# Two chunks of P moved to a load's wait; at the start, one cast given to ACT and the state's transposes split over two tiles

## Chip, cores, metric

One core of one Trainium2 chip. The metric is the device time of the whole kernel in microseconds (us); smaller is better. Where a run is traced, the profile's span is about 1.7 us shorter than the time of the same run.

## The reference, cut to what matters

```python
# x: [8, 8, 512, 64], state: [8, 8, 32, 64], w_in: [512, 2048], w_out: [2048, 512]
a     = softmax(scale * x @ state.T)        # per batch and head
xread = a @ state                           # 512 rows a batch
sread = softmax(scale * state @ x.T) @ x    # 32 rows a batch
y     = concat([xread, sread]) -> [8 * 544, 512]
out   = gelu(y @ w_in) @ w_out
```

The kernel never forms `xread`. It computes P = state @ w_in for each batch (2 x 128 rows by 2048 columns, in four chunks of 512), and then h = a @ P. So P chunks (batch b, quarter f) are small matmuls that must lie somewhere ahead of the h matmuls that read them. This is what the change moves.

## The kernel before

The program gives the order on each engine by itself; nothing is rescheduled. `M(i)` is one h tile (two full matmuls, then Gelu on ACT), `U(i)` and `mm2_m` are second-layer matmuls into `op`. PSUM has four banks for everything tagged `f`, taken in rotation, and four tagged `op`, which hold the open sums of batch 0.

```python
def scores(b, half):                       # tag f, freed by Exp on ACT
    pt = ps_f.tile([128, SJ, 2, 2, NS], FP32, name="pt", tag="f")
    ...                                    # 8 matmuls
    nc.scalar.activation(out=A.e[...], in_=pt..., func=AF.Exp, scale=scale)

def p_mm(b, f, pool, tag):                 # a chunk: 2 tiles, 8 matmuls of 64*32
    ps = [pool.tile([128, 512], FP32, name="p_ps", tag=tag) for t in range(2)]
    for c in range(HC):
        for t in range(2):
            nc.tensor.matmul(ps[t][32 * c:32 * c + 32, :], ...)
    return ps

def p_copy(b, f, ps):                      # each tile freed by its own engine
    dst = Ps[b][:, :, f * 512:(f + 1) * 512]
    nc.scalar.copy(out=dst[:, 0, :], in_=ps[0])
    nc.vector.tensor_copy(out=dst[:, 1, :], in_=ps[1])
...
    # start: batch 0
    keep_warm(32); cast0(0); xtr0(0)
    st0 = state0()        # 4 transposes + 1, one tile; ACT copies to sb0
    cast0(1); state0_p(st0); keep_warm(5)
    cast0(2); xtr0(1); xtr0(2); xtr0(3)
    scores0(0); ...
...
    # around the third w_out chunk (m = 8..11)
    xtr(1, (0, 1)); xtr(1, (2, 3)); rearr_ones(1)
    M(10, 11)
    mm2_m(0, 8)                            # first use of that chunk
    scores(1, 0); scores(1, 1)
    mm2_m(0, 9)
    burst([(0, 3), (1, 0)])
    norm(1, 0); norm(1, 1)                 # softmax on DVE
    mm2_m(0, 10); mm2_m(0, 11); M(12, 13); M(14, 15)
    ...
    sread(1); sread_out(1)                 # tile sr, freed by DVE's srm
    burst([(1, 1), (1, 2)])
    atr(1); U(12); srt(1); state_prep(2, B); U(13); M(16, 17); ...
```

The softmax here doesn't subtract the row's maximum and nothing guards it: scores larger than these inputs give would overflow.

Of the kernel before, what the change touches and what calls it, by code (L numbers as in the profile page):

```python
# [10 lines left out]
BF16 = mybir.dt.bfloat16  # L11
# [6 lines left out]
def kernel(  # L18
# [8 lines left out]
    nc = tc.nc  # L27

    B, H, S, D = x.shape
    _, _, NS, _ = state.shape  # L30
# [3 lines left out]
    HC = H // 2  # L34
# [10 lines left out]
    ps_f = ctx.enter_context(tc.tile_pool(name="ps_f", bufs=4, space=PSUM))  # L45
# [9 lines left out]
    sbd = persist.tile([128, B, HC, 2 * NS], BF16, name="sbd")  # L55
# [8 lines left out]
    sb0 = persist.tile([128, 2, 2, 2, NS], BF16, name="sb0")  # L64
# [80 lines left out]
    def keep_warm(n, m=128):  # L145
        for _ in range(n):
            nc.tensor.matmul(
                warm_ps[0:m, 0:128], lhsT=warm[:, 0:m], rhs=warm, start=True, stop=True
            )
# [20 lines left out]

    def state0():
        nc.scalar.copy(out=st_bf[:, 0, :, :], in_=st_f)
        ps = ps_f.tile([128, 3, HC, NS], BF16, name="st0_ps", tag="f")
        for t in range(2):
            for u in range(2):
                nc.tensor.transpose(
                    ps[64 * u:64 * u + 64, t, :, :].rearrange("p c n -> p (c n)"),
                    st_bf[:, 0, t, :],
                    ident,
                )  # L180
        nc.tensor.transpose(
            ps[:, 2, :, :].rearrange("p c n -> p (c n)"),
            st_bf[:, 0, :, :].rearrange("q t d -> q (t d)"),
            ident,
        )
        for u in range(2):
            h = slice(64 * u, 64 * u + 64)
            nc.scalar.copy(out=sb0[h, :, :, u, :], in_=ps[h, 0:2, u:HC:2, :])
        return ps

    def state0_p(ps):
        for t in range(2):
            h = slice(64 * t, 64 * t + 64)
            nc.scalar.copy(out=sbd[h, 0, :, 32 * t:32 * t + 32], in_=ps[h, 2, :, :])


    class Att:
# [28 lines left out]
    def rearr_ones(b):  # L226
        A = atts[b]
        eng = nc.vector if b < 2 else nc.gpsimd
        src = xbs[b].rearrange("p (t c) (j d) -> p t c j d", t=2, d=D)
        for t in range(2):  # L230
            eng.tensor_copy(  # L231
                out=A.xo[:, :, :, 2 + 64 * t:66 + 64 * t].rearrange("p j c d -> p c j d"),
                in_=src[:, t],
            )


    def cast0(q):
        nc.vector.tensor_copy(
            out=x0b[:, q, :, :, :].rearrange("p j u d -> p u j d"),
            in_=x0f[:, q, :, :].rearrange("p u (j d) -> p u j d", d=D),  # L240
        )
# [11 lines left out]
    def xtr0(q):  # L253
        ps = ps_f.tile([128, SJ, 128], BF16, name="xT_ps", tag="f")
        for j in range(SJ):
            if q < 3:
                nc.tensor.transpose(
                    ps[:, j, :], x0b[:, q, j, :, :].rearrange("p u d -> p (u d)"), ident
                )
                continue  # L260
            for u in range(2):
                nc.tensor.transpose(
                    ps[64 * u:64 * u + 64, j, :], x0c[:, u, D * j:D * j + D], ident
                )
        nc.vector.tensor_copy(out=xT0[:, q, :, :], in_=ps)
# [85 lines left out]
    def scores(b, half):  # L351
        A = atts[b]
        pt = ps_f.tile([128, SJ, 2, 2, NS], FP32, name="pt", tag="f")
        for ci in range(2):
            c = 2 * half + ci
            for j in range(SJ):
                nc.tensor.matmul(  # L357
                    pt[:, j, :, ci, :],
                    lhsT=A.xT[:, j, c, :],
                    rhs=sbd[:, b, c, :],  # L360
                    start=True,
                    stop=True,
                )
        nc.scalar.activation(  # L364
            out=A.e[:, :, 64 * half:64 * half + 64],
            in_=pt.rearrange("p j t c n -> p (j t) (c n)"),
            func=AF.Exp,
            scale=scale,
        )
# [17 lines left out]
    def atr(b, ts=(0, 1)):  # L387
        A = atts[b]
        if 0 in ts:
            A.AT = att.tile([128, SJ, 2, 128], BF16, name="AT", tag="AT")  # L390
        for t in ts:
            ps = ps_f.tile([128, SJ, 128], BF16, name="aT_ps", tag="f")
            for j in range(SJ):
                nc.tensor.transpose(ps[:, j, :], A.a[:, 2 * j + t, :], ident)
            nc.vector.tensor_copy(out=A.AT[:, :, t, :], in_=ps)
# [9 lines left out]
    def sread(b):  # L405
        A = atts[b]
        pool, tag = (ps_o, "op") if b == B - 1 else (ps_f, "f")
        A.sr = pool.tile([128, 2, 65], FP32, name="sr", tag=tag)
        for t in range(2):
            for j in range(SJ):  # L410
                for c in range(HC):
                    nc.tensor.matmul(  # L412
                        A.sr[32 * c:32 * c + 32, t, :],
                        lhsT=A.e[:, 2 * j + t if b else SJ * t + j, 32 * c:32 * c + 32],
                        rhs=A.xo[:, j, c, 1 + 65 * t:66 + 65 * t],
                        start=(j == 0),
                        stop=(j == SJ - 1),
                    )

    def sread_out(b):  # L420
        A = atts[b]
        A.srm = att.tile([128, 2, D], BF16, name="srm", tag="srm")
        flat = A.sr.rearrange("q t d -> q (t d)")
        inv = att.tile([128, 2], FP32, name="inv", tag="inv")
        nc.vector.reciprocal(out=inv, in_=flat[:, 0:130:129])
        nc.vector.tensor_tensor(
            out=A.srm,
            in0=flat[:, 1:129].rearrange("q (t d) -> q t d", t=2),
            in1=inv[:, :].to_broadcast((128, 2, D)),
            op=ALU.mult,  # L430
        )
# [11 lines left out]
    def p_mm(b, f, pool, tag):  # L443
        if b not in Ps:
            Ps[b] = att.tile([128, 2, d_ff], BF16, name="P", tag="P")
# [3 lines that stand above are left out]
                nc.tensor.matmul(  # L449
                    ps[t][32 * c:32 * c + 32, :],  # L450
                    lhsT=sbd[64 * t:64 * t + 64, b, c, 32 * t:32 * t + 32],
                    rhs=w_in_bf[64 * t:64 * t + 64, c, f * 512:(f + 1) * 512],
                    start=True,
                    stop=True,
                )
        return ps

    def p_copy(b, f, ps):
# [3 lines that stand above are left out]
# [7 lines left out]
    def burst(chunks, reads=()):  # L469
        done = []  # L470
        first = len(chunks) < 4
        if first:
            for b in reads:
                sread(b)
        for i, (b, f) in enumerate(chunks):
            pool, tag = (ps_f, "f") if i < 2 else (ps_o, "op")
            done.append((b, f, p_mm(b, f, pool, tag)))
        for x in done[:2]:
            p_copy(*x)
        if not first:  # L480
            for b in reads:
                sread(b)
        for x in done[2:3]:
            p_copy(*x)
        for b in reads:
            sread_out(b)
        for x in done[3:]:
            p_copy(*x)
# [114 lines left out]
    def mm2_m(b, m):  # L603
        for j in range(SJ):
            if m == 0:
                ops[b, j] = ps_o.tile([128, d_model], FP32, name="op", tag="op")
            nc.tensor.matmul(  # L607
                ops[b, j],
                lhsT=gs[b][:, m, j * 128:(j + 1) * 128],
                rhs=w_out_bf[:, m, :],  # L610
                start=(m == 0),
                stop=(m == MC - 1),
            )


    def M(*ms):
        for m in ms:
            mm1(m // MC, m % MC)

    def U(*us):  # L620
        for u in us:
            mm2(u // 16, u % 16 // 4, u % 4)

    begin(0)
    keep_warm(32)
    cast0(0)
    xtr0(0)
    st0 = state0()
    cast0(1)
    state0_p(st0)  # L630
    keep_warm(5)
    cast0(2)
    xtr0(1)
    xtr0(2)
    xtr0(3)
    scores0(0)
# [44 lines left out]
    begin(1)  # L681
    xtr(1, (0, 1))
    xtr(1, (2, 3))
    rearr_ones(1)
    M(10, 11)
    mm2_m(0, 8)
    scores(1, 0)
    scores(1, 1)
    mm2_m(0, 9)
    burst([(0, 3), (1, 0)])  # L690
    norm(1, 0)
    norm(1, 1)
    mm2_m(0, 10)
# [7 lines left out]
    rearr_ones(2)  # L701
    sread(1)
    sread_out(1)
    burst([(1, 1), (1, 2)])
    atr(1)
    U(12)
    srt(1)
    state_prep(2, B)
    U(13)
# [8 lines left out]
    u = 17  # L718
# [77 lines left out]
```

## Time and profile before

Median 216.37 us (216.16 to 216.68, 4 runs). PE is busy for 98% of the span. Three spots matter, in us from the span's start:

| what | where | size |
|---|---|---|
| PE's weight loads wait for batch 1's x, ahead of its transposes | 23.49 | 0.33 as the profile counts it; the matmuls 0.07 |
| PE waits for the third w_out chunk | 25.54 to 26.45 | 0.91 |
| PE waits inside the burst (1,1),(1,2) for PSUM banks | ends 34.37 | 0.81 as the profile counts it |

The prediction shows the lines for these. In the timeline, a row is start, busy time, engine, line, operation, tiles, forms, count, and in brackets the idle time before it. A row's busy time has holes in it if matmuls of the group waited: this is how the bank wait looks in PE's timeline of the kernel before.

```profile
33.37 1.41 PE L449 MATMUL p_ps<-w_in_bf,sbd 64*32 64x512 bf16 x16
34.70 0.64 PE L394 MATMUL aT_ps<-ident,a 128*128 128x128 bf16 x8
```

Sixteen P matmuls take from 33.37 to 34.70 here, and about 0.6 where nothing holds them. Two banks hold them in turn: the ninth matmul starts alone at 33.94, 0.06 after Gelu of m=15 ends (33.88), and the last seven at 34.37, after DVE's srm (34.31).

```profile
23.07 0.22 PE L156 MATMUL st_ps<-ident,st_bf 128*128 128x128 bf16 x1
23.22 1.08 PE L279 MATMUL xT_ps<-ident,xb 128*64 128x128 bf16 x32
```

### The profile page before, as it was taken

How to read it: one execution, taken by the hardware profiler on the slowest of the kernel's cores; microseconds unless marked ns; L12 is line 12 of the kernel's file. 1: busy time of each engine (PE TensorE's matmuls, PEld its weight loads, DVE VectorE, ACT ScalarE, POOL GpSimd, SP SyncE). 2: the span in 40 equal slices, each digit the busy share in tenths (PEclk: the TensorE clock that was granted, in tenths of full speed). 3: DMA queues.
4: the chain of work that ended last, by engine and by line, in shares of the span. 5: the costliest groups of instructions: out<-in, count | busy, mean ns of one | idle time of the engine just before them, and what ended most of it. 6: DMA issues, size and time to landing. Idle time of an engine off the chain costs nothing.

```text
span 214.9 us, 4080 instructions
## 1 busy us (share of the span) xinstructions
PE 209.7 (98%) x1700; PEld 103.1 (48%) x1700; DVE 79.8 (37%) x173; ACT 121.9 (57%) x216; POOL 43.5 (20%) x58
## 2 busy tenths in 40 slices
PE   8999899999999999999999999999999999999994
PEld 7634444444545444444444454444444444765443
DVE  4721559723049302850078005910393025000151
ACT  2754685696676447944874477645954444864000
POOL 7935204901113013301312121300000000000000
PEclk9999999999999999999999999999999999999999
DMA  6999999992723492428540872261232004000044
GB/s 183 183 203 194 207 190 150 197 244 52 98 98 101 81 143 41 177 41 134 74 173 25 148 96 108 90 129 20 77 123 52 0 26 173 0 0 3 6 106 181
DMA packets 41187, 23.24 MB, mean 108 GB/s; under 512 B 23120, under 2 KB 37712, under 8 KB 41168
## 3 DMA queue, kind: packets, MB, share of 16 engines
q0 software_dynamic: 14208, 8.23, 28.0%
q1 hardware_dynamic: 26272, 14.36, 24.8%
q10 hardware_dynamic: 688, 0.39, 0.6%
q8 instruction: 13, 0.21, 0.4%
q14 instruction: 6, 0.05, 0.1%
HBM read 17.30 MB, written 8.91 MB: 122 GB/s over the span
## 4 chain that ended last, share of the span: by engine, by line
PE 84%; DMA 10%; DVE 2%; POOL 2%; issue 1%; ACT 0%; POOLq 0%
PE op L562 45%; PE hp L513 23%; DMA w_out_bf<-in_moe_w_out_dram 10%; PE p_ps L449 4%; PE hps L577 3%; PE ops L589 3%; PE opl L540 2%; PE pt L357 2%; PE sr L412 1%; POOL w_in_bf L101 1%; PE op L607 1%; DVE a L380 1%; DVE P L461 1%; DVE cs L377 1%; POOL x0c L85 0%
## 5 line engine op out<-in xcount | busy, mean ns | idle before, releaser
L562 PE MATMUL op<-w_out_bf,g 128*128 128x512 bf16 x448 | 106.3, 379 | 0.0
L520 ACT ACTIVATE g<-hp 128x512 bf16<-128x512 f32 x124 | 66.4, 599 | 54.8 <-PE hp L513 54.7
L562 PEld LDWEIGHTS <-g 128*128 128x128 bf16 x448 | 43.6, 98 | 51.9 <-issue 0.8
L513 PE MATMUL hp<-AT,P 128*128 128x512 bf16 x248 | 63.1, 379 | 0.0
L526 DVE COPY osb<-op 128x512 f32<-128x512 f32 x31 | 21.4, 692 | 83.3 <-PE op L562 83.2
L513 PEld LDWEIGHTS <-P 128*128 128x128 bf16 x248 | 23.1, 98 | 26.0 <-ACT P L460 0.4
L461 DVE CAST P<-p_ps 128x512 bf16<-128x512 f32 x31 | 20.0, 683 | 12.4 <-PE p_ps L449 12.3
L460 ACT CAST P<-p_ps 128x512 bf16<-128x512 f32 x31 | 16.4, 595 | 12.5 <-PE p_ps L449 12.5
L221 POOL COPY x<-xb 128x1024 bf16<-128x1024 bf16 x12 | 12.1, 1041 | 33.3 <-DMA xb<-in_x_dram 28.3
L231 POOL COPY xo<-xb 128x1024 bf16<-128x1024 bf16 x12 | 12.2, 1046 | 21.3 <-PE sr L412 21.3
L607 PE MATMUL op<-w_out_bf,g 128*128 128x512 bf16 x48 | 11.5, 380 | 1.0 <-DMA w_out_bf<-in_moe_w_out_dram 0.9
L449 PE MATMUL p_ps<-w_in_bf,sbd 64*32 64x512 bf16 x248 | 11.0, 381 | 0.1
L377 DVE TENSOR_REDUCE cs<-e 128x16 f32<-128x512 bf16 x14 | 9.5, 677 | 3.7 <-ACT e L364 3.7
L380 DVE TENSOR_TENSOR a<-e,ics 128x512 bf16<-128x512 bf16 x14 | 9.7, 692 | 0.5
L364 ACT ACT_TABLE_LOAD x7 | 9.0, 1283 | 1.4 <-issue 1.3
L526 DVE COPY osb<-ops 128x512 f32<-128x512 f32 x2 | 1.4, 692 | 22.5 <-PE ops L589 22.5
L520 ACT ACT_TABLE_LOAD x7 | 9.0, 1283 | 0.1
L551 ACT COPY osb<-opl 128x128 f32<-128x128 f32 x1 | 0.3, 266 | 15.2 <-PE opl L540 15.2
L364 ACT ACTIVATE e<-pt 128x512 bf16<-128x512 f32 x14 | 7.6, 594 | 0.3 <-PE pt L357 0.2
L577 PE MATMUL hps<-XSR,w_in_bf 128*128 128x256 bf16 x64 | 7.6, 273 | 0.0
L607 PEld LDWEIGHTS <-g 128*128 128x128 bf16 x48 | 4.3, 98 | 7.0 <-issue 2.1
L449 PEld LDWEIGHTS <-sbd 64*32 64x32 bf16 x248 | 3.5, 89 | 7.6 <-issue 5.6
(85 smaller groups left out, 122.9 us busy)
## 6 DMA issues: line engine op xcount, KB each, us to landing
out_dram<-osb SPq DMA_DIRECT2D x25, 256.0 KB, 2.3
xb<-in_x_dram POOLq DMA_DIRECT2D x7, 512.0 KB, 6.3
w_out_bf<-in_moe_w_out_dram POOLq DMA_DIRECT2D x4, 512.0 KB, 11.9
w_in_bf<-in_moe_w_in_dram POOLq DMA_DIRECT2D x6, 256.0 KB, 11.8
out_dram<-osb SPq DMA_DIRECT2D x12, 128.0 KB, 2.1
x0f<-in_x_dram SPq DMA_DIRECT2D x2, 256.0 KB, 3.3
w_in_bf<-in_moe_w_in_dram POOLq DMA_DIRECT2D x4, 128.0 KB, 4.5
out_dram<-osb SPq DMA_DIRECT2D x8, 64.0 KB, 1.7
```

The source lines that it names most:

```text
L221: nc.gpsimd.tensor_copy(out=A.x4[:, :, :, 64 * t:64 * t + 64].rearrange("p j c d -> p c j d"), in_=src[:, t],)
L231: eng.tensor_copy(out=A.xo[:, :, :, 2 + 64 * t:66 + 64 * t].rearrange("p j c d -> p c j d"), in_=src[:, t],)
L364: nc.scalar.activation(out=A.e[:, :, 64 * half:64 * half + 64], in_=pt.rearrange("p j t c n -> p (j t) (c n)"), func=AF.Exp, scale=scale,)
L449: nc.tensor.matmul(ps[t][32 * c:32 * c + 32, :], lhsT=sbd[64 * t:64 * t + 64, b, c, 32 * t:32 * t + 32], rhs=w_in_bf[64 * t:64 * t + 64, c ...
L460: nc.scalar.copy(out=dst[:, 0, :], in_=ps[0])
L461: nc.vector.tensor_copy(out=dst[:, 1, :], in_=ps[1])
L513: nc.tensor.matmul(hp, lhsT=Ps[b][:, t, m * 128:(m + 1) * 128], rhs=atts[b].AT[:, :, t, :], start=(t == 0), stop=(t == 1),)
L520: nc.scalar.activation(out=gs[b][:, m, :], in_=hp, func=AF.Gelu)
L526: nc.vector.tensor_copy(out=osb, in_=ps)
L562: nc.tensor.matmul(ps, lhsT=gs[b][:, m, j * 128:(j + 1) * 128], rhs=w_out_bf[:, m, :], start=(m == 0), stop=(m == MC - 1),)
L577: nc.tensor.matmul(hp, lhsT=w_in_bf[:, c, m * 128:(m + 1) * 128], rhs=XSR[:, c, :], start=(c == 0), stop=(c == HC - 1),)
L607: nc.tensor.matmul(ops[b, j], lhsT=gs[b][:, m, j * 128:(j + 1) * 128], rhs=w_out_bf[:, m, :], start=(m == 0), stop=(m == MC - 1),)
```

## The change

The intent: put independent work, chunks (1,0) and (1,1), where PE stands waiting for w_out; drop the later burst that ran into held banks, by giving its chunk (1,2) to the burst of (0,3); and shorten the start by giving one of batch 0's casts to ACT and by splitting the state's transposes over two tiles, so that scores need not wait for all five.

```diff
     # start
-        ps = ps_f.tile([128, 3, HC, NS], ...)      # 5 transposes, one tile
+        ps = ps_f.tile([128, 2, HC, NS], ...)      # 4 transposes; the fifth in state0_p
...
-        nc.vector.tensor_copy(                     # cast0
+        copy = nc.scalar.copy if q == 1 else nc.vector.tensor_copy
+        copy(
...
-    state0_p(st0)
-    keep_warm(5)
+    state0_copy(st0)
+    keep_warm(6)
     cast0(2)
     xtr0(1)
+    state0_p()
     xtr0(2)
...  # P chunks
-    rearr_ones(1)
     M(10, 11)
+    burst([(1, 0), (1, 1)])
     mm2_m(0, 8)
     scores(1, 0)
     scores(1, 1)
+    rearr_ones(1)
     mm2_m(0, 9)
-    burst([(0, 3), (1, 0)])
+    burst([(0, 3), (1, 2)])
...
     sread_out(1)
-    burst([(1, 1), (1, 2)])
+    U(12)
     atr(1)
-    U(12)
     srt(1)
```

More of the change, by code (lines that the diff above doesn't have):

```diff
@@ L172, in state0 @@
         nc.scalar.copy(out=st_bf[:, 0, :, :], in_=st_f)
-        ps = ps_f.tile([128, 3, HC, NS], BF16, name="st0_ps", tag="f")
+        ps = ps_f.tile([128, 2, HC, NS], BF16, name="st0_ps", tag="f")
         for t in range(2):
@@ L180, in state0, with state0_copy, state0_p @@
                 )
+        return ps
+    def state0_copy(ps):
+        for u in range(2):
+            h = slice(64 * u, 64 * u + 64)
+            nc.scalar.copy(out=sb0[h, :, :, u, :], in_=ps[h, :, u:HC:2, :])
+    def state0_p():
+        ps = ps_f.tile([128, HC, NS], BF16, name="st0p_ps", tag="f")
         nc.tensor.transpose(
-            ps[:, 2, :, :].rearrange("p c n -> p (c n)"),
+            ps.rearrange("p c n -> p (c n)"),
             st_bf[:, 0, :, :].rearrange("q t d -> q (t d)"),
@@ L185, in state0 @@
         )
-        for u in range(2):
-            h = slice(64 * u, 64 * u + 64)
-            nc.scalar.copy(out=sb0[h, :, :, u, :], in_=ps[h, 0:2, u:HC:2, :])
-        return ps
-    def state0_p(ps):
         for t in range(2):
             h = slice(64 * t, 64 * t + 64)
-            nc.scalar.copy(out=sbd[h, 0, :, 32 * t:32 * t + 32], in_=ps[h, 2, :, :])
+            nc.scalar.copy(out=sbd[h, 0, :, 32 * t:32 * t + 32], in_=ps[h, :, :])
     class Att:
```

## The prediction

> **What bounds the kernel now.** I read the page first, then the chain of work that ended last, then the timeline engine by engine up to 46 us, and last the landing times of the loads from the views of their tiles. The page's first part and three rows of the view of stretches say it in short:
>
> ```profile
> PE 209.7 (98%) x1700; PEld 103.1 (48%) x1700; DVE 79.8 (37%) x173; ACT 121.9 (57%) x216; POOL 43.5 (20%) x58
> ...
> 10.60:25.50 14.90, 14.86 (x109) 6.42 (x106) 4.54 (x12) 7.62 (x16) 5.67 (x8) 1.00 1.29 201
> 25.50:26.50 1.00, 0.09 (x2) 0.04 (x1) 0.63 (x2) 0.98 (x3) 0.00 (x0) 1.00 1.25 212
> 26.50:34.40 7.90, 7.76 (x104) 3.35 (x103) 4.83 (x11) 7.03 (x11) 0.00 (x0) 1.00 1.53 193
> ```
>
> The columns are the stretch, its length, then busy time of PE, weight loads, DVE, ACT and POOL, the clock, the DMA share and GB/s. PE is busy in every stretch except 25.5 to 26.5 us, and the DMA engines are full throughout (about 200 GB/s). From 37.3 us to the end the chain is PE alone, back to back, so a matmul that starts x earlier at 37 us makes the kernel x shorter. The question is only what the change is worth between 0 and 37 us. The pieces of the chain that decide it, and the waits behind them:
>
> ```profile
> 12.20 14.22 DMA w_out_bf<-in_moe_w_out_dram
> 26.41 0.04 issue
> 26.45 1.02 PE op L607 x4
> ```
>
> ```profile
> PEld L449 <- DVE srm L426: 0.8, 1, 0.8
> PE op L607 <- DMA w_out_bf<-in_moe_w_out_dram: 0.9, 1, 0.9
> ```
>
> ```profile
> 26.25 1.28 ACT L364 ACT_TABLE_LOAD   x1
> 27.75 1.08 ACT L364 ACTIVATE e<-pt 128x512 bf16<-128x512 f32 x2 [0.21 <-PE pt L357]
> 29.36 1.07 ACT L460 CAST P<-p_ps 128x512 bf16<-128x512 f32 x2 [0.53 <-PE p_ps L449]
> 30.45 1.28 ACT L520 ACT_TABLE_LOAD   x1
> ```
>
> PE waits in two places. At 25.54 it waits 0.91 us for the third w_out chunk, issued at 12.20 and landed at 26.41. In the later burst of P chunks (1,1) and (1,2), which starts at 33.37, it stands still until 34.37: the last of that burst's four PSUM tiles takes the buffer that sread's result holds until DVE has written srm, and DVE is late because of the softmax work before it. ACT, 7.03 us busy of 7.90, is the second thing to watch in that stretch.
>
> **What the Trainium skill says.** (1) "ScalarE: Activation LUTs", section "What ACT_TABLE_LOAD costs": about 1283 ns for a switch of set, and a drain of about 1380 ns on top. The trace agrees with the first (1.28 us) and not with the second: the load at 30.45 ends at 31.73 and Gelu starts at 31.82. Copies load no table here (the casts at 29.36 follow Exp directly). (2) "TensorE: Matmul & The Clock Gate", section "Part 3: Packing small matmuls": small matmuls in different array tiles run together. The trace agrees: the 16 P matmuls of two chunks advance the chain by 0.57 us, while one full 128x512 matmul takes 0.216 (0.86 for four). (3) "Perfetto Trace Analysis", section "Matmuls": independent groups should rotate through different PSUM banks, so that evacuation overlaps the next group. Here four banks rotate under tag f, and the stall at 33.94 to 34.37 is what it looks like when the next bank in turn is still held. (4) The same page, section "Optimizing Scalar/DVE Operations": some operations can be done by either engine. A 128x512 cast took 0.43 us on DVE from SBUF and 0.60 on ACT from PSUM, so the swap is a matter of who is free.
>
> **Part one, the start (0 to 10.6 us).** Today DVE casts q=1 at 5.39 (0.68 us), only after it has copied xT of q=0. The row of x landed about 4.95 (issued at 1.25, 3.7 to land). Now ACT does it after the state's cast, some 4.98 to 5.58, so it is ready about 0.45 us earlier. The fifth state transpose leaves the first tile, so the two ACT copies into sb0 wait for less, and the copies into sbd come after xtr0(1). PE then reaches xtr0(1) at about 5.95 and not 6.13 (the end of six warm-up matmuls at 0.107 each from 5.30), and the first scores at about 6.95 and not 7.11. Exp and everything behind it comes about 0.15 to 0.2 us earlier. I expect this to be visible, and then to be lost twice:
>
> ```profile
> 15.32 0.65 PE L449 MATMUL p_ps<-w_in_bf,sbd 64*32 64x512 bf16 x8
> 21.19 0.41 PE L449 MATMUL p_ps<-w_in_bf,sbd 64*32 64x512 bf16 x8
> ...
> 23.49 1.08 PE L275 MATMUL xT_ps<-ident,xb 128*64 128x128 bf16 x32
> ```
>
> The same 8 matmuls took 0.65 at 15.32 and 0.41 at 21.19: the second half of w_in's second quarter was issued at 6.54 and takes 9.0 us to land, so at 15.5. And xb of batch 1, issued at 9.78, lands 13.7 us later, at 23.48; the transposes start at 23.49. Both loads are set by a full DMA queue and not by PE. So the gain of the start adds **0** to the end.
>
> **Part two, the P chunks.** I follow the four buffers of tag f in their order of allocation, as the program gives it; for the kernel before, this rule gives the wait at 34.37 correctly, which is why I trust it.
> - Burst (1,0),(1,1) at 25.38 (PE's issue is free one pitch before the modelled end, 25.54). Its four tiles take the buffers of the two transposes of x (the last copied at 25.46) and of hp 10 and 11. The Gelu of hp 11 ends at 26.23, so the last tile's first matmul starts at 26.29, and the rest takes what it took after 34.37 before (0.33 until the next matmul): PE is free at **26.62**. The w_out chunk is there at 26.41. So mm2 of m=8 starts 0.17 later than today's 26.45, with two chunks already done.
> - ACT now has two casts (1.08) ahead of the table load: 26.25 to about 27.40, load to 28.68, two Exp (1.08 and its start gap) to **29.84**, where today they end at 28.83. That is 1.0 us later, though ACT's waits of 0.21 and 0.53 today are used up.
> - Burst (0,3),(1,2): PE is there at 26.62 + 0.86 + 0.47 + 0.86 = 28.81. The first two tiles are free (casts done 27.4). The next two are those of the scores, free after each Exp: the last at 29.88, plus 0.33: PE is free at **30.21**, today 29.45. This is a new wait of about 0.8 us.
> - From there today's work runs unchanged but for the second burst: 29.45 to 36.44 (start of U(13)) is 6.99 us, of which the burst of 33.37 to 34.70 is 1.33. It is gone now: 30.21 + 6.99 - 1.33 = **35.87**, today 36.44. Saved: 0.57 us.
> - Checks on the way: a table load for Gelu after the casts at 30.4 to 30.95 ends at 32.2, before hp 12 is done (32.5). Gelu of m=15 ends about 34.63, and U(12), which comes earlier now, needs it at 34.77. Softmax ends on DVE at about 34.28 and its transposes come at 34.98. The AT copies end at 36.6 and M(16) asks for them at 36.7. The fourth w_out chunk (issued at 18.75, 12.4 to land) is there at 31.15. These margins are 0.1 us in two places, so I take off another 0.05.
>
> Sum: 0.00 (start) - 0.52 = **215.9 us** from 216.39 (0.52 = 0.57 - 0.05, rounded in the total).
>
> **The rivals.**
> A, *the wait is simply filled*: both waits vanish, 0.91 + 0.72 (1.33 less the 0.6 of a burst that doesn't wait), less the little that the first burst overruns. This makes 215.0. For it: both are plain in the waits. Against it: the burst needs four PSUM tiles, two of which are held by Gelu and then by Exp, and ACT gets its Exp a microsecond later.
> B, *the new wait eats it all*: if Exp came later still than 29.84 (ACT behind the last cast, or a drain at the table load as the skill has it), the burst of (0,3) and U(12) would slip, and the time is 216.4 or a little over. For it: ACT is 7.03 of 7.90 us busy here. Against it: the trace shows no drain.
> C, *the start carries through*: if the loads came sooner too, another 0.15 to 0.2 would be kept: 215.7. For it: one cast less on DVE beside POOL's issues. Against it: the loads already move 182 GB/s in the first 5 us, near the 200 of later.
>
> **Range and chances.** My own sum has four links of about 0.1 us each and one (the Exp path) of perhaps 0.3; the kernel's own runs lie within 0.33 us (216.35 to 216.68). So 215.4 to 216.3, with A and C below or at the lower end and B at the upper. 2% is 4.3 us; all PE idle time in the first 37 us comes to less than that, and nothing adds as much. So within 2%: 0.98, faster 0.01, slower 0.01.
>
> **What would show each step right or wrong.** In the changed profile: the wait of PE on w_out_bf is gone or under 0.1 us; P matmuls start near 25.4; PE idles some 0.8 us near 29.1 to 29.9, released by ACT's Exp; the table load for Exp begins near 27.4 and not 26.25; no wait of weight loads on srm; the first scores near 6.95, yet mm1 after 23.49 where it was; U(13) near 35.9. I am wrong if the Exp wait is missing (A), if there is a new idle time of more than 0.2 us between 31 and 37 us (B), or if xb's transposes start before 23.4 (C).

## More of the kernel before

From the scores of batch 2 (45.08) to the end, PE runs without holes; 169.8 us pass from there to the end of the span. Only what happens before is at stake.

## The result, and the profile after

Median 215.96 us (215.69 to 216.04, 4 runs) against 216.37 us. The ratio is 0.9978, 95% interval 0.996 to 0.9995. Ratios here are the mean time of one kernel's fast runs over that of the other's fast runs of the same rounds, so not quite the ratio of the medians quoted. The kernel is a little faster, well within 2%, and the prediction of 215.9 with its range of 215.4 to 216.3 holds.

The view of stretches of the changed kernel, with the columns of the prediction's first fence (the row from 26.50 is to be held against the same row of before):

```profile
25.50:26.50 1.00, 0.88 (x17) 0.34 (x16) 0.45 (x2) 1.00 (x3) 0.00 (x0) 1.00 1.25 212
26.50:34.40 7.90, 7.73 (x95) 3.44 (x91) 6.21 (x13) 7.42 (x12) 0.00 (x0) 1.00 1.52 193
```

PE's hole for w_out is filled: 0.88 us busy and not 0.09. Yet ACT has become almost full (7.42 of 7.90), and busy time on PE hides what the timeline of PE shows:

```profile
23.57 1.08 PE L279 MATMUL xT_ps<-ident,xb 128*64 128x128 bf16 x32
...
25.55 1.22 PE L453 MATMUL p_ps<-w_in_bf,sbd 64*32 64x512 bf16 x16
26.70 1.04 PE L611 MATMUL op<-w_out_bf,g 128*128 128x512 bf16 x3
...
29.00 1.26 PE L453 MATMUL p_ps<-w_in_bf,sbd 64*32 64x512 bf16 x16
30.20 1.90 PE L611 MATMUL op<-w_out_bf,g 128*128 128x512 bf16 x8
```

Both bursts take about 1.2 us from start to the next group, where 0.6 is their work: each waits for PSUM banks. The chain of work that ended last goes through these holes, and says who holds the banks:

```profile
25.23 1.09 ACT g L524 x2
26.36 0.47 PE p_ps L453 x7
26.83 0.57 ACT P L464
27.43 1.28 ACT L368
28.72 1.09 ACT e L368 x2
29.86 0.41 PE p_ps L453 x7
```

Gelu of the last two h tiles frees the first burst; ACT then copies, loads the Exp table (27.43), runs Exp to 29.80, and only this frees the second burst. Before, the table load began at 26.25. The wait for w_out and the wait on srm are gone, and two bank waits of about 0.6 us stand in their place. (In this trace's list of waits they show only as idle time of weight loads put down to "issue", 2.1 us in six pieces for L453, without the name of who held the bank. The hole in the timeline shows them, and the chain names who held the bank.)

### The profile page after: what moved, and what is told of

It is laid out like the page before. It is cut to its first block, busy times and chain, and to the rows that moved or that the text cites. A ratio compares the mean times of both kernels' runs of the same rounds, so it can differ in the third digit from the quotient of the medians.

```text
span 214.3 us, 4058 instructions
## 1 busy us (share of the span) xinstructions
PE 208.6 (97%) x1676; PEld 103.4 (48%) x1701; DVE 79.9 (37%) x172; ACT 122.2 (57%) x217; POOL 43.4 (20%) x58
## 4 chain that ended last, share of the span: by engine, by line
PE 96%; ACT 2%; issue 1%; DVE 0%
PE op L566 45%; PE hp L517 25%; PE p_ps L453 4%; PE op L611 4%; PE hps L581 3%; PE ops L593 3%; PE warm_ps L147 2%; PE opl L544 2%; PE sr L416 1%; PE pt L361 1%; PE hp L664 1%; ACT L368 1%; PE xT_ps L261 1%; PE rb L337 1%; ACT e L368 1%
## 5 line engine op out<-in xcount | busy, mean ns | idle before, releaser
L566 PE MATMUL op<-w_out_bf,g 128*128 128x512 bf16 x426 | 104.1, 379 | 1.2
L566 PEld LDWEIGHTS <-g 128*128 128x128 bf16 x448 | 43.5, 98 | 52.1 <-issue 0.8
L611 PE MATMUL op<-w_out_bf,g 128*128 128x512 bf16 x45 | 11.4, 380 | 0.2
L453 PE MATMUL p_ps<-w_in_bf,sbd 64*32 64x512 bf16 x248 | 11.3, 381 | 0.3
L453 PEld LDWEIGHTS <-sbd 64*32 64x32 bf16 x248 | 3.7, 89 | 8.5 <-issue 7.5
L593 PE MATMUL ops<-w_out_bf,g_sr 128*128 128x512 bf16 x32 | 7.1, 379 | 0.0
```

What stands on the lines that cost most here:

```text
L453: nc.tensor.matmul(ps[t][32 * c:32 * c + 32, :], lhsT=sbd[64 * t:64 * t + 64, b, c, 32 * t:32 * t + 32], rhs=w_in_bf[64 * t:64 * t + 64, c ...
L566: nc.tensor.matmul(ps, lhsT=gs[b][:, m, j * 128:(j + 1) * 128], rhs=w_out_bf[:, m, :], start=(m == 0), stop=(m == MC - 1),)
L593: nc.tensor.matmul(ps, lhsT=g_sr[:, m, s * 128:(s + 1) * 128], rhs=w_out_bf[:, m, :], start=(m == 0), stop=(m == MC - 1),)
L611: nc.tensor.matmul(ops[b, j], lhsT=gs[b][:, m, j * 128:(j + 1) * 128], rhs=w_out_bf[:, m, :], start=(m == 0), stop=(m == MC - 1),)
```

## The experiments

The loads do not land at the same moment in each run, so spans alone mix two things. The table splits each trace: the first scores of batch 0, the x transposes of batch 1, and the time from these transposes to the scores of batch 2. The rest is 169.8 us in all. What sets the x transposes is a load further ahead: in ten of the twelve traces PE comes to the P matmuls near 15 us before the second half of w_in's second quarter has landed, and waits (0.25 us in before, 0.42 in changed). From the group after those matmuls (15.91 in before, 16.05 in changed) to the x transposes pass 7.5 to 7.6 us in every trace, so that batch 1's x itself adds 0.1 us at most.

| kernel | first scores | x transposes | from there to batch 2's scores | span |
|---|---|---|---|---|
| before | 7.11 | 23.49 | 45.08 - 23.49 = 21.59 | 214.9 |
| changed | 7.15 | 23.57 | 20.90 | 214.3 |
| p_only | 7.03 | 23.34 | 20.90 | 214.0 |
| start_only | 7.14 | 23.53 | 21.28 | 214.6 |
| slow_start | 7.42 | 23.46 | 20.90 | 214.1 |
| late12 | 6.71 | 23.35 | 21.09 | 214.2 |
| after_again (changed, again) | 6.74 | 22.74 | 20.91 | 213.4 |
| dve11 | 6.70 | 23.22 | 20.28 | 213.3 |
| late14 | 6.75 | 23.30 | 20.89 | 214.0 |
| before_split | 7.04 | 23.48 | 21.75 | 215.0 |
| dve11_again | 6.85 | 23.78 | 20.29 | 213.9 |
| dve11_oldstart | 7.04 | 23.23 | 20.43 | 213.4 |

The theory: the P moves give all of the gain, less a new wait for Exp; the start gives none. The rivals: the start gives part; the load alone sets the stage; the srm wait alone was the loss.

### p_only and start_only: each part by itself

The P hunks of the diff on the old start, and the start hunks with the old P order.

> Only the moves of the P chunks, the start as in the kernel before. Theory (the start is worth nothing, loads pin PE at the second quarter of w_in and at batch 1's x): the time of the changed kernel, 0.998 of before, that is 0.4 to 0.5 us less; U(13) starts near 35.8 us. Rival (the start carries through): about 0.15 to 0.2 us slower than the changed kernel.

> Only the new start, the P chunks as in the kernel before. Theory: the time of the kernel before, within 0.1 us (ratio 1.000); the wait for w_out at 26.4 is back at about 0.9 us. Rival (the start carries through, or all of the gain is of the start): 0.2 to 0.5 us less.

p_only: 216.26 us, ratio 0.9976 (0.9955 to 0.9996). start_only: 216.56 us, ratio 0.9994 (0.9977 to 1.0011). The first has the 20.90 us stage of the whole change, the second stands where the kernel before does. The times alone (intervals of some 0.4 us either way) would not rule out 0.2 us for the start; these traces give it no place, see the next run. One detail missed: start_only's wait for w_out was 0.4 us and not 0.9, as the chunk landed sooner in that run. Of the 0.5 us, 0.2 went again in the burst behind it (0.91 to the next group and not 0.71), which waited for the last part of w_in; so its stage is 21.28 and not 21.59. The gain of the P moves therefore depends on a load's luck: 0.69 us against the trace of before (21.59 - 20.90), 0.38 against this one.

### slow_start: a start made worse on purpose

```diff
-    keep_warm(6)
+    keep_warm(12)
```

> The changed kernel with six more warm-up matmuls at the start, on PE ahead of batch 0's transposes: PE's start is 0.64 us later (6 x 0.107). Theory: the two waits for loads (0.42 us inside the P matmuls at 15.3, 0.26 at 23.6) swallow it, so the time is that of the changed kernel to within 0.1 us, and the x transposes of batch 1 still start at 23.5 to 23.6. Rival (the start is on the path): 0.64 us slower.

215.82 us, ratio 0.9963 (0.9945 to 0.9981): no slower than the changed kernel. PE's timeline:

```profile
6.55 0.41 PE L261 MATMUL xT_ps<-ident,x0b 128*128 128x128 bf16 x4
...
15.58 0.43 PE L453 MATMUL p_ps<-w_in_bf,sbd 64*32 64x512 bf16 x8
...
23.46 1.08 PE L279 MATMUL xT_ps<-ident,xb 128*64 128x128 bf16 x32
```

The P matmuls at 15.58 find w_in landed and run through in 0.43 (0.83 in the changed kernel, which came at 15.29 and waited), and the x transposes start at 23.46 as ever. The six extra matmuls delayed the first scores by 0.27 us rather than 0.64, because the transposes after them ran faster (0.41 for four, not 0.63; the last section returns to it). So the test was milder than planned, but a delay of 0.27 us vanished in the wait for w_in. In these traces the start is off the path. It would not have swallowed more: PE came as the load had just landed, and took 0.36 to the next group, where 0.34 to 0.35 is the time of a chunk that nothing holds.

### late12: chunk (1,2) away from Exp

```diff
-    burst([(0, 3), (1, 2)])
+    burst([(0, 3)])
...
     U(12)
+    burst([(1, 2)])
     atr(1)
```

> The changed kernel with chunk (1,2) taken out of the burst that waits for Exp, and put after U(12). Theory (the new wait for Exp's PSUM tiles takes back about 0.8 us): the wait near 29.1 to 29.9 goes, ACT goes straight to its Gelu, U(13) starts near 35.2 to 35.3 and not 35.83, the time is about 0.5 us less than the changed kernel, 215.4. Rival (the DMA alone sets it, the Exp wait is of no account): the time of the changed kernel.

216.01 us, ratio 0.9968 (0.9951 to 0.9985): no gain over the changed kernel (0.9978 and 0.9965 in its two sets of runs, neither of the same rounds), and the stage is 21.09 us, 0.19 longer. The expectation failed, and PE's timeline says why:

```profile
28.78 0.41 PE L453 MATMUL p_ps<-w_in_bf,sbd 64*32 64x512 bf16 x8
29.12 1.90 PE L611 MATMUL op<-w_out_bf,g 128*128 128x512 bf16 x8
...
34.35 0.62 PE L398 MATMUL aT_ps<-ident,a 128*128 128x128 bf16 x8
35.12 0.22 PE L440 MATMUL srT<-ident,srm 128*128 128x128 bf16 x1
35.46 0.49 PE L156 MATMUL st_ps<-ident,st_bf 128*128 128x128 bf16 x6
```

The Exp wait did go: the chunk takes 0.34 to the next group. But srT and st_ps are the next two tiles in the rotation, and their banks are those of chunk (1,2), whose copies end at 35.06 on ACT and 35.40 on DVE. They start 0.06 after each, 0.3 us late twice. I had followed the banks up to the chunk and not beyond it. The copy on DVE was itself queued behind the eviction of U(12).

### dve11: Exp one copy earlier, PE's order untouched

```diff
-        nc.scalar.copy(out=dst[:, 0, :], in_=ps[0])
+        (nc.vector.tensor_copy if (b, f) == (1, 1) else nc.scalar.copy)(out=dst[:, 0, :], in_=ps[0])
```

> The changed kernel once more, unchanged, as the yardstick on the same chip as the other three: 0.4 to 0.5 us less than before, U(13) near 35.8 us in the trace.

> The changed kernel, but both copies of chunk (1,1) on DVE, so that ACT reaches its table load and Exp one cast (0.57 us) earlier; order on PE untouched. Theory (PE waits for Exp to give back its PSUM tiles): the wait inside the P matmuls at 29.0 shrinks from 0.85 to about 0.25 us, U(13) starts near 35.2 and not 35.83, the time is about 0.6 us less than the changed kernel. Rival (that wait is hidden or set by something else, DVE's copies or the w_in load for chunk (0,3)): the time of the changed kernel or more, with the wait still at 29.4.

after_again: 215.81 us, ratio 0.9965 (0.9945 to 0.9986), 0.75 less than before by medians. Its trace has U(13) at 35.00 and not near 35.8, though its stage is 20.91 as ever: it is ahead from the x transposes on, which start at 22.74. Here the second half of w_in's second quarter landed at 14.84 (issued at 6.44, 8.4 to land), so PE, which came at 14.88, did not wait for it:

```profile
14.88 0.42 PE L453 MATMUL p_ps<-w_in_bf,sbd 64*32 64x512 bf16 x8
...
22.59 0.22 PE L156 MATMUL st_ps<-ident,st_bf 128*128 128x128 bf16 x1
22.74 1.08 PE L279 MATMUL xT_ps<-ident,xb 128*64 128x128 bf16 x32
```

In this one trace nothing swallows the start. The four traces with the old start come to these matmuls at 15.17 to 15.32, so the old start would have cost some 0.3 to 0.4 us here. That is an estimate from these times; no run pairs the two starts under such an early landing.

dve11: 215.31 us, ratio 0.9941 (0.9923 to 0.9959). In the trace of dve11:

```profile
28.24 0.59 ACT L368 ACTIVATE e<-pt 128x512 bf16<-128x512 f32 x1
28.65 0.65 PE L453 MATMUL p_ps<-w_in_bf,sbd 64*32 64x512 bf16 x16
...
29.23 1.04 PE L611 MATMUL op<-w_out_bf,g 128*128 128x512 bf16 x4
```

The second Exp starts at 28.24, so ends at 28.83, before its bank is asked for. The burst now takes 0.58 to the next group, where it took 1.20 (29.00 to 30.20). That is 0.62 us, and the stage shrinks by 20.90 - 20.28 = 0.62. Nothing on PE was moved. So the wait for Exp is shown, with its size, and DVE had the room.

### late14: chunk (1,2) still later

As late12, but with the chunk after U(14), where the next users of its banks are further off.

```diff
-    burst([(0, 3), (1, 2)])
+    burst([(0, 3)])
...
     U(14)
+    burst([(1, 2)])
     M(18, 19)
```

> The run before that put (1,2) after U(12) lost the Exp wait but got two new ones: the transposes of srm and of the state waited 0.3 us each for the two copies of (1,2) to free their PSUM tiles. Here (1,2) comes after U(14), where the next users of those tiles are a matmul group away. Theory: no Exp wait, no wait on srm, no wait at the transposes: U(13) near 34.9 with 0.3 us of P matmuls still to come, so 0.6 to 0.7 us less than the changed kernel, near 215.3. Rival (something else holds the end back): no gain over the changed kernel.

215.53 us, ratio 0.9953 (0.9933 to 0.9972); its interval overlaps that of after_again, and its stage, 20.89 us, is that of the changed kernel. Two things ate the gain:

```profile
28.73 0.81 PE L453 MATMUL p_ps<-w_in_bf,sbd 64*32 64x512 bf16 x8
29.46 1.90 PE L611 MATMUL op<-w_out_bf,g 128*128 128x512 bf16 x8
...
36.82 1.03 PE L566 MATMUL op<-w_out_bf,g 128*128 128x512 bf16 x4
37.78 0.41 PE L453 MATMUL p_ps<-w_in_bf,sbd 64*32 64x512 bf16 x8
38.12 1.04 PE L517 MATMUL hp<-AT,P 128*128 128x512 bf16 x4
```

Chunk (0,3) takes 0.73 to the next group and not 0.34: the last part of w_in, issued at 15.68 and 13.4 us in landing, is there only at 29.1. That is this run's landing: in late12 it was there at 28.7, before the chunk began (28.78). Where PE waits for Exp such a landing is covered: in after_again it came at 28.6, 0.4 us into the burst, and the stage is 20.91 all the same. Still, PE is free 6.16 us after the x transposes (29.46 - 23.30), against 6.63 (30.20 - 23.57): 0.47 saved. And the chunk by itself costs 0.44 (36.82 to 38.12 is 1.30, a U group alone 0.86), where two chunks in one burst cost 0.68 (27.69 to 29.23 in dve11, less 0.86). So 0.47 - 0.44 leaves 0.03. I had counted 0.3 for the chunk and nothing for w_in; with w_in in time late14 would have been some 0.4 us shorter (an estimate: 0.73 - 0.34).

### before_split: take away the wait on srm alone

The kernel before, with its second burst cut in two and put after U(14) and after M(18, 19).

```diff
     sread_out(1)
-    burst([(1, 1), (1, 2)])
     atr(1)
...
     U(14)
+    burst([(1, 1)])
     M(18, 19)
+    burst([(1, 2)])
     U(15)
```

> The kernel before, with its chunks (1,1) and (1,2) moved from before the transposes of a to after U(14) and after M(18,19); the start and the wait for w_out untouched. It takes away the wait on srm alone. Theory: that wait (0.7 to 0.8 us) goes and none takes its place, so 0.7 us less than before, more than the change itself brought, though PE still waits 0.9 us for w_out. Rival (the gain can only come from filling the wait for w_out): the time of the kernel before.

216.99 us (216.23 to 218.25), ratio 1.0025 (0.9998 to 1.0052): no gain, if anything slower. The waits of this kernel between 25 and 38 us:

```profile
PEld L394 <- DVE a L380: 0.6, 1, 0.6
...
PE aT_ps L394 <- DVE a L380: 0.5, 1, 0.5
...
PE op L607 <- DMA w_out_bf<-in_moe_w_out_dram: 0.5, 1, 0.5
```

With the burst gone, PE reaches the transposes of `a` sooner and waits 0.5 us for DVE's softmax. So the wait on srm stood in front of another wait on the same engine's queue. And the split bursts each paid for themselves: 0.44 us for (1,1) (37.28 to 38.58, less 0.86 for the U group) and 0.58 for (1,2) (38.58 to 40.02, less 0.86 for the h group). The burst had cost 1.33 us; 0.52 + 0.44 + 0.58 is more than that. (Taking the burst away also took away its wait for Gelu, so the wait on srm was not removed alone.) It takes the U(12) put ahead of the transposes, as the change has it, to give DVE that time: in the changed kernel atr starts at 34.99, 0.7 after `a` is done (DVE's next instruction starts at 34.28), and no such wait is listed. This run does not test that U(12) by itself; it stays an argument from the trace.

### dve11 again, and with the old start

> The best version so far once more (both copies of chunk (1,1) on DVE), with another kernel beside it: 0.994 of before, 0.5 to 0.6 us less than the changed kernel; 20.3 us from the x transposes of batch 1 to the scores of batch 2, where the changed kernel has 20.9 and the kernel before 21.6 (less if w_out lands sooner).

> The same with the start of the kernel before. Theory (the start is worth nothing, as the load of batch 1's x holds PE at 23.3 to 23.6 either way): the same time as the one beside it, within 0.2 us, and 20.3 us from the x transposes to the scores of batch 2. Rival (where the loads come early, the new start does carry through): 0.2 to 0.4 us slower, with no wait for batch 1's x ahead of its transposes.

dve11_again: 215.46 us, ratio 0.9943 (0.9922 to 0.9963), stage 20.29. dve11_oldstart: 215.28 us, ratio 0.9942 (0.9924 to 0.996), stage 20.43 with 0.14 in its burst at 28.66 (0.79 busy, not 0.65), as the last part of w_in landed at 28.8 there. The two are the same. So the best version found is the P moves plus one copy on DVE, 1.05 to 1.25 us under the kernel before by medians, and no gain of the new start shows beside it.

## Why the prediction was right, and where it was not

- **The first burst and the load.** Put at 26.62 for mm2 of m=8; measured 26.70, with the x transposes 0.08 late themselves. Right, including that the burst overruns the load because it waits for Gelu.
- **ACT pushed back.** Table load put at 27.40, measured 27.43; Exp ended at 29.80, put at 29.84. Right.
- **The new wait.** PE free at 30.21 by the working, 30.20 in the trace; dve11 took this wait away and got 0.62 us back. Right, and shown as the cause, not only seen. The 0.8 us that the text gives it is the last tile's wait as against before; in the burst, the hole is 0.62. (The 0.57 us that the prediction reads for sixteen P matmuls is, in the chain, a piece of eight, 28.81 in the kernel before; sixteen with nothing to hold them took 0.58 in dve11, so the figure was right by chance.)
- **The later part.** U(13) put at 35.87, measured 35.83. The margins of 0.1 us held: the last weight load of U(12) idles 0.24 us before Gelu lets it go, yet U(12) takes 0.88 and not 0.86.
- **The start.** That it adds nothing to the end held in start_only, slow_start and dve11_oldstart. The reason is half right: the wait for w_in swallows it, and not that for batch 1's x, which the prediction read from the weight loads (0.33 us) where the matmuls lost 0.07. And it holds only while w_in lands late, which it did not in after_again. That the first scores would come at 6.95 failed in the profiled run: 7.15, as xtr0(1) began when it was put (5.92) but four transposes took 0.42 us from start to start, where I had reckoned about 0.3. start_only had 7.14, but in five other traces with the new start they came between 6.70 and 6.85. The working took PE's pace there for fixed, and it is not. As the step lies ahead of the wait for w_in, its error cost nothing.
- **The sum.** Minus 0.5 predicted; measured 0.41 by medians in one set, and 0.75 for the repeat (216.56 - 215.81). What the working missed is that the time before isn't one number: with the old order the w_out wait was 0.9 us in before, 0.4 in start_only and 0.5 in before_split. The eleven or twelve runs of before on each chip lie within 1.0 to 1.2 us, where the prediction took 0.33. So that U(13) came within 0.04 us is luck in part: the loads landed at nearly the same times in the two traces, but U(13) came at 35.00 in after_again.
- **The rivals.** A (both waits vanish) fell to the two bank waits. B (a drain makes Exp later still) fell: Exp starts at 28.72, 0.01 after the table load ends. C (the start carries through) has no place in the medians, as far as 0.2 us can be told (start_only, dve11_oldstart), but its condition, loads that come sooner, was met in after_again, where nothing swallows the start. The sign that the prediction set for C, x transposes before 23.4, came in six traces, two of them with the old start (p_only 23.34, dve11_oldstart 23.23): it tells when w_in landed, not which start ran.

## What to carry to other kernels

Filling a wait for a load with other work is worth the wait less what the filler holds: here four PSUM banks and a slot in ACT's queue, so that of the 1.63 us in two waits (0.91 + 0.72, as the prediction counts them) 0.94 came back, mostly as waits for banks, and 0.69 was kept. A late load swallows what is gained ahead of it, but only in the runs in which it is late, so compare several traces before calling such a gain nothing. Follow the rotation of the banks past the moved work to its next users, because two moves that looked free (late12, before_split) only handed the wait on. And before moving anything, look whether the slack engine can take one instruction from the tight one: one copy from ACT to DVE brought more than the start and as much again as the move of the chunks.

## What the Trainium skill lacked or had wrong

- "TensorE: Matmul & The Clock Gate", section "What you observe": about 107 ns a 128-column matmul until about 4 us of activity, 56 ns after, give or take 500 ns between runs. The first pace agrees: 32 warm-up matmuls took 3.60 us in the chain of the changed kernel, up to its first transpose (about 0.11 each). But the switch came at two quite different times for the same start: in the changed kernel four transposes of x took 0.63 us both at 4.38 and at 5.92, in late12 0.40 us at 4.28 already. So full pace came within 3.3 us of PE's first matmul (0.99), or only after 5 us of nearly unbroken work. The half microsecond that the section gives is too narrow here, and the profile's granted clock, 1.00 for both, doesn't show it.

```profile
4.38 0.63 PE L261 MATMUL xT_ps<-ident,x0b 128*128 128x128 bf16 x4
...
5.92 0.63 PE L261 MATMUL xT_ps<-ident,x0b 128*128 128x128 bf16 x4
```

  Those two are the changed kernel's; this one is late12's:

```profile
4.28 0.40 PE L261 MATMUL xT_ps<-ident,x0b 128*128 128x128 bf16 x4
```

- "ScalarE: Activation LUTs", section "What ACT_TABLE_LOAD costs": the drain of about 1380 ns beside the load is not seen; 0.01 us lies between the load's end and Exp in the changed kernel (27.43 + 1.28, then 28.72), and 0.02 between the last copy (26.20 + 1.21) and the load.
- "TensorEngine Tiling (Array Packing)", section "Key Properties": a change of tiling mode drains TensorE, but neither this page nor another gives the time that it costs to go from full-size matmuls to a burst of packed ones and back. Here a lone chunk of eight cost 0.44 us in late14, two together 0.68 in dve11, so some 0.2 us (0.44 x 2 - 0.68) for splitting one burst in two. That a drain is the cause is not shown.
- No page has the spread of a load's landing in the same program: the third w_out chunk was there at 26.4 us in the traces of before and after, and at 25.98 or sooner in start_only, where PE began on it at 25.98 after waiting. Over all twelve traces it came between 25.3 (after_again, 11.91 + 13.4) and 26.7 us (dve11_again, 12.31 + 14.4).
